# A gated recurrence and a low-rank mixer on one core: another common order of all operations, and unread matrix products joined up to 512 columns

## The chip, the core and the metric

The kernel runs on one core of a Trainium2 chip. The core has five engines, each with its own queue that it works through in order: TensorE (PE, matrix products, written to the accumulation memory PSUM; its weight loads are shown apart as PEld), VectorE (DVE, elementwise work), ScalarE (ACT, functions and copies), GpSimd (POOL) and SyncE (SP, which here issues most transfers). Transfers (DMA) move data between device memory and the on-chip memory, or within the latter. The metric is the device time of one execution in microseconds (us), the median of several runs.

## The reference

Two parts follow each other. The first is a recurrence over 768 steps with a complex decay per channel, for 4 sequences with 8 heads of 48 channels:

```python
mag = np.sqrt(a_re * a_re + a_im * a_im)
scale = np.minimum(mag, 0.999) / (mag + 1e-06)
a_re_n, a_im_n = (a_re * scale, a_im * scale)
for t in range(S):
    ar, ai = (a_re_n[:, :, t, :, None], a_im_n[:, :, t, :, None])
    new_re = ar * S_re - ai * S_im
    new_im = ar * S_im + ai * S_re
    kv = np.einsum('bhd,bhe->bhde', k[:, :, t], v[:, :, t])
    S_re, S_im = (new_re + kv, new_im)
    y[:, :, t] = np.einsum('bhd,bhde->bhe', q[:, :, t], S_re)
```

The second takes y as x, with 384 channels, mixes along the sequence through rank 32, and then applies two dense layers with a hidden width of 1536:

```python
xt = x.transpose(0, 2, 1)
h = xt @ U @ V
u = x + h.transpose(0, 2, 1)
ch = np.maximum(u @ w_ch1, 0.0) @ w_ch2
return (u + ch).astype(np.float32)
```

The weights and the low-rank factors come in double precision; the kernel makes single precision of them with integer operations on VectorE and ScalarE.

## The kernel before

The 4 x 768 steps are cut into 24 chunks of 128 steps, two to a group. For each group, `gates` (line 596) loads a_re and a_im (`load_a`, line 511), forms the logarithm of the decay in the tile GL (ScalarE and VectorE in turn, lines 624 to 645), and sums it along the chunk by matrix products with constant triangular matrices: "es ps" with `mid` and "ef ps" with `fore` (line 674, or line 670 for later groups, where the values are split in two). The exponentials of these sums weigh q and k. `of_blocks` gives sums over blocks ("tot", lines 712 and 718), which SyncE's transfers bring into the tile T (line 696). `turns_of` and `angles` do the same for the phase ("ph", lines 773 to 779, F at line 782), and `waves_of` makes cosine and sine of it.

For each chunk, `prep` (line 811) weighs q and k and transposes them on TensorE ("tr", line 834; copied out by ScalarE, line 845). `chain` (line 856) then forms products within blocks of 32 steps ("inner", lines 881 and 884), masks them into DG (line 896), copies their diagonal blocks into AT with four transfers (line 935), adds off-diagonal blocks ("corners", line 948), forms the state ("dk", line 973) and the output y (lines 1004 and 1012).

When a sequence's six chunks are done, `mixer` (line 1028) runs for its three pairs of chunks: "rank" and "mixed" for the low-rank part (lines 1047, 1066), a transposition (line 1079), the first dense layer ("up", line 1094, or, for the last five of the twelve pairs, "few" of line 1152, a scheme with fewer products and more additions), and the second ("down", lines 1241 and 1284). Weights are loaded and converted by `single` (line 529) on the side.

The order is written out. Every operation is recorded with `plan.add` under an engine and a kind; the table `ORDER` (line 28) gives for each kind and running number one place among 2,655 places that all engines share. `Plan.order` sorts by place and asserts that an operation comes after what it needs and that buffers are free; the operations are then emitted in this order, and each engine's instructions keep it. Which engine waits for which data at run time follows from the tiles that an instruction reads and writes, not from the table. The costs in the code (`c_act`, `c_dve`, `c_dma` and the numbers in `PE(...)`) are not used in `Plan.order`.

A second table, `SPARE` (line 175), puts matrix products that nobody reads in front of the operation at a given place: `ident` times `ident` into a PSUM tile "spare" of its own (line 1414), 128 columns each.

```python
out += [-1] * SPARE.get(at[n], 0) + [n]
```

Of the kernel before, what the change touches and what calls it, by code (L numbers as in the profile page):

```python
# [10 lines left out]
FP = mybir.dt.float32  # L11
# [26 lines left out]
    ("POOL", "load"): {0: [13], 1.5: [59], 2: [12], 1: [28]},  # L38
    ("DVE", "load"): {1: [40]},
# [6 lines left out]
    ("ACT", "gates"): {0: [0, 7, 6, 11, 16, 21, 23, 36, 53, 43, 44, 45, 55, 58], 1: [14, 8, 22, 29, 30, 37, 46, 54, 48, 49, 52, 57], 2: [127, 104,  # L46
# [10 lines left out]
    ("DVE", "gates"): {0: [10, 9, 17, 25, 27, 63, 24], 1: [15, 26, 33, 35, 38, 64, 41], 2: [117, 144, 151, 186], 4: [261, 313, 314, 352], 6: [427,  # L57
# [10 lines left out]
    ("ACT", "angles"): {0: [78, 87, 92, 93, 100], 1: [84, 101, 107, 111, 110], 2: [197, 202, 220, 236, 232, 238, 239, 246, 248, 249], 4: [363, 376,  # L68
# [5 lines left out]
    ("DVE", "angles"): {0: [81, 82, 90], 1: [85, 88, 103], 2: [201, 231, 245], 4: [375, 395, 419], 6: [563, 567, 571, 592, 599, 600, 636], 8: [672,  # L74
# [5 lines left out]
    ("DVE", "prep"): {0: [91, 102, 112], 1: [116, 124, 138], 2: [240, 254, 257], 3: [241, 275, 306], 4: [402, 407, 425], 5: [424, 432, 464], 6: [608,  # L80
# [159 lines left out]
def kernel(  # L240
# [24 lines left out]
    nc = tc.nc  # L265
# [44 lines left out]
    plan = Plan(places)  # L310
# [717 lines left out]
    def mixer(m):  # L1028
# [220 lines left out]
        def down_two():  # L1249
# [29 lines left out]
            def product(to, part, x, y, reads, first=True):  # L1279
# [6 lines left out]
                for half in range(2):  # L1286
                    PE(0.98, RM, lambda half=half: products(half), reads(half) + [("w2s", 0)],
                       [to + (part,), ("bank", to[1])], steps=KH)
# [181 lines left out]
```

## Time and profile before

| What | Value |
|---|---|
| median of 3 runs | 640.84 us (638.37 to 641.07) |
| the profiled execution: first to last instruction | 641.9 us |
| TensorE busy | 622.8 us in 10,516 product records |
| VectorE, ScalarE, GpSimd busy | 509.9, 396.8, 38.7 us |
| unread products (line 1414) | 294 records, 43.9 us busy, from 1.4 to 125.7 us |
| "up" of line 1094, weight loads apart | 504 records, 116.1 us busy |
| mean granted clock of TensorE | 0.992 of full speed |

A product of full-precision numbers shows as two records of the same shape. A row of the timeline gives its start, its length, engine and line, what is written from what, shapes, the number of records, and in brackets the idle time of the engine before it and what ended that. A row of waits gives who waited for whom, the time in total, how often, and the longest. A row of stretches gives, after the stretch and its length, the busy time of each engine with its records, then the granted clock as a share of full speed, the share of the transfer engines that was busy, and GB/s. The chain is the work that ended last, followed back from the end; its rows are start, length and work. TensorE's ends are modelled, so that records of one run overlap a little.

Every transfer of a_re, a_im, q, k or v is 192 KB, an issue on SyncE takes some 0.4 to 0.9 us, and the median time from issue to landing is 3.2 to 3.4 us. An AT<-DG transfer is 32 KB and lands in 2.4 us at the median.

### The profile page before, as it was taken

The page shows a single profiled execution, that of the slowest core. Times are in us where ns is not written, and L with a number is a line of the kernel's source. Part 1 is how long each engine was busy: PE and PEld are TensorE (multiplying, and loading weights), DVE is VectorE, ACT ScalarE, POOL GpSimd, SP SyncE. Part 2 cuts the span into 40 slices and gives each one's busy share as a digit, 9 for nine tenths or more (in the row PEclk, how much of TensorE's full clock was granted, in tenths as well). Part 3 has the DMA queues.
Part 4 walks back from the last instruction along what each step waited for, and adds up shares of the span by engine and source line. Part 5 has one row for each costly group of instructions (what it writes and reads, how often), then busy time and mean ns, then how long its engine had stood idle before and what let it go on. Part 6 is the DMA issues. An engine that isn't in the chain of part 4 may idle for free.

```text
span 641.9 us, 23713 instructions
## 1 busy us (share of the span) xinstructions
PE 622.8 (97%) x10516; PEld 548.0 (85%) x10516; DVE 509.9 (79%) x923; ACT 396.8 (62%) x765; POOL 38.7 (6%) x79
## 2 busy tenths in 40 slices
PE   8888997999999999999999999999999999999998
PEld 7767776686789988889988989798999998999997
DVE  6998997678999989678877868788999975473743
ACT  7898997788887787876776676687532432102020
POOL 5000000000001010010010100010000000000001
PEclk9999999799999999999999999999999999999999
DMA  7766534745233362333331332611104010000002
GB/s 202 166 148 138 125 70 102 180 119 131 51 66 69 58 126 50 67 69 68 71 77 34 75 74 43 117 37 21 32 20 81 8 42 12 7 1 1 20 1 74
DMA packets 173686, 45.76 MB, mean 71 GB/s; under 512 B 167632, under 2 KB 170384, under 8 KB 173584
## 3 DMA queue, kind: packets, MB, share of 16 engines
q1 hardware_dynamic: 171376, 39.90, 29.4%
q0 software_dynamic: 2208, 4.35, 2.0%
q8 instruction: 82, 1.34, 0.9%
q14 instruction: 20, 0.16, 0.1%
HBM read 33.59 MB, written 4.72 MB: 60 GB/s over the span
## 4 chain that ended last, share of the span: by engine, by line
PE 72%; issue 9%; ACT 7%; DMA 6%; DVE 4%; SPq 3%; POOL 0%; DVEq 0%; ACTq 0%; POOLq 0%
PE down L1284 22%; PE up L1094 11%; PE few L1152 10%; PE y L1012 3%; DMA AT<-DG 3%; PE tr L834 3%; PE dk L973 3%; PE down L1241 3%; ACT gate L374 2%; PE y L1004 2%; PE inner L884 2%; PE inner L881 2%; PE mixed L1066 1%; PE spare L1414 1%; PE tot L718 1%
## 5 line engine op out<-in xcount | busy, mean ns | idle before, releaser
L1094 PE MATMUL up<-uT,w 128*128 128x256 f32 x504 | 116.1, 383 | 0.0
L377 DVE TENSOR_TENSOR QK<-QK,T 112x512 f32<-112x512 f32 (+2 forms) x144 | 101.3, 728 | 7.1 <-PE corners L948 2.6
L1094 PEld LDWEIGHTS up<-uT,w 128*128 128x128 f32 x504 | 93.8, 190 | 12.8
L374 ACT ACTIVATE gate<-gate 128x768 f32<-128x768 f32 (+1 forms) x89 | 70.1, 798 | 8.1 <-DVE GS L768 3.1
L1284 PE MATMUL down<-w,h 128*128 128x192 f32 x396 | 73.5, 331 | 0.0
L845 ACT COPY QK<-tr 112x512 f32<-112x512 f32 x96 | 53.2, 584 | 32.2 <-PE tr L834 31.8
L1284 PEld LDWEIGHTS down<-w,h 128*128 128x128 f32 x396 | 64.1, 190 | 2.7 <-issue 1.5
L1160 ACT COPY h<-few 128x512 f32<-128x512 f32 x30 | 17.3, 586 | 60.9 <-PE few L1152 60.9
L380 DVE TENSOR_TENSOR xo<-down,xo 128x192 f32<-128x192 f32 (+1 forms) x79 | 29.9, 384 | 26.5 <-PE down L1284 26.3
L377 DVE TENSOR_TENSOR QKC<-qk,cs 128x768 f32<-128x768 f32 x48 | 45.4, 952 | 5.2 <-PE tr L834 4.5
L1414 PE MATMUL spare<-ident 128*128 128x128 f32 x294 | 43.9, 295 | 1.4 <-POOL ident masks.py:199 1.4
L1414 PEld LDWEIGHTS spare<-ident 128*128 128x128 f32 x294 | 38.1, 200 | 6.0 <-issue 2.0
L1284 PE MATMUL down<-stage 128*128 128x192 f32 x198 | 37.2, 331 | 0.0
L1152 PE MATMUL few<-gate,w 128*128 128x128 f32 x280 | 35.4, 276 | 0.0
L834 PEld LDWEIGHTS tr<-ident,QKC 64*112 64x112 f32 x768 | 25.9, 130 | 10.7 <-issue 3.3
L834 PE MATMUL tr<-ident,QKC 64*112 64x64 f32 x768 | 33.1, 223 | 1.9 <-ACT QK L845 0.8
L759 POOL DMA_DIRECT2D gate<-F x15 | 11.9, 796 | 379.1 <-DVE F L782 225.3
L1152 PEld LDWEIGHTS few<-gate,w 128*128 128x128 f32 x280 | 33.4, 192 | 0.1
L1284 PEld LDWEIGHTS down<-stage 128*128 128x128 f32 x198 | 32.1, 190 | 1.5 <-DVE stage L1276 0.6
L953 ACT COPY AT<-corners 32x128 f32<-32x128 f32 x96 | 24.2, 255 | 12.1 <-PE corners L948 10.5
L371 ACT ACT_TABLE_LOAD x24 | 30.8, 1283 | 1.1 <-PEq L1454 0.7
L1228 POOL DMA_DIRECT2D out_dram<-xo x32 | 18.5, 606 | 207.2 <-DVE xo L380 119.6
(156 smaller groups left out, 1245.9 us busy)
## 6 DMA issues: line engine op xcount, KB each, us to landing
stage<-in_moe_w_ch_dram SPq DMA_DIRECT2D x12, 768.0 KB, 4.7
gate<-in_a_im_dram SPq DMA_DIRECT2D x24, 192.0 KB, 3.3
gate<-in_a_re_dram SPq DMA_DIRECT2D x24, 192.0 KB, 3.2
VP<-in_v_dram SPq DMA_DIRECT2D x24, 192.0 KB, 3.4
qk<-in_k_dram SPq DMA_DIRECT2D x24, 192.0 KB, 3.3
qk<-in_q_dram SPq DMA_DIRECT2D x24, 192.0 KB, 3.3
AT<-DG SPq DMA_DIRECT2D x96, 32.0 KB, 2.4
T<-E SPq DMA_DIRECT2D x48, 48.0 KB, 2.5
```

The lines of the kernel that those rows point to most:

```text
L371: ACT(1.37, rank, lambda: nc.scalar.preload_act_table_set(name), writes=[TABLE])
L374: return nc.scalar.activation(out=o, in_=i, func=f, **kw)
L377: nc.vector.tensor_tensor(out=o, in0=a, in1=b, op=OP.mult)
L380: nc.vector.tensor_tensor(out=o, in0=a, in1=b, op=OP.add)
L834: nc.tensor.transpose(out=get(*ps[r])[0:DQ, h], in_=get(*qkc)[at, h].rearrange("p u d -> p (u d)")[:, 0:DQ], identity=ident[at, at], tile_ ...
L845: nc.scalar.copy(out=to, in_=a)
L953: ACT(0.36, RR, lambda r=r, u=u: nc.scalar.copy(out=get(*ATi).rearrange("p (a u) t -> p a u t", u=2)[r:r + BLK, :, u, BLK:2 * BLK], in_=ge ...
L973: nc.tensor.matmul(out=get(*dk[r])[x:end, h], lhsT=get(*ks)[at, h, x // DP, 0:end - x], rhs=get(*VPi)[at, h], start=True, stop=True, tile_ ...
L1094: nc.tensor.matmul(out=get(*ps)[:, e], lhsT=w1[:, f, (ff + e) * 128:(ff + e + 1) * 128], rhs=get(*uT)[:, f], start=(f == 0), stop=(f == KD ...
L1152: nc.tensor.matmul(out=get(*ps)[:, q], lhsT=w()[:, q * 128:(q + 1) * 128], rhs=v[0](), start=(n == 0 and q == 0), stop=True, skip_group_ch ...
L1284: nc.tensor.matmul(out=get(*to)[:, part], lhsT=x(j), rhs=y[:, j], start=(first and j == 0), stop=(j == KH - 1), skip_group_check=not first)
L1414: nc.tensor.matmul(out=spare[0], lhsT=ident, rhs=ident, start=True, stop=True)
```

## The change

All places in `ORDER` are new, for all engines and queues: the same operations with the same arguments, in another order. `SPARE` is new. Runs of unread products are joined by four into one product of up to 512 columns, whose right-hand side repeats `ident`. The second layer's products name all of w2 as read when the plan is made. There is no other edit.

The places of the first gate operations before and after (each entry is a place; the key is the chunk):

```diff
-    ("ACT", "gates"): {0: [0, 7, 6, 11, 16, 21, 23, 36, 53, 43, 44, 45, 55, 58], 1: [14, 8, 22, 29, 30, 37, 46, 54, 48, 49, 52, 57], 2: [127, 104,
+        ("ACT", "gates"): {0: [1, 4, 2, 6, 12, 13, 15, 35, 48, 42, 39, 44, 68, 76], 1: [8, 14, 24, 25, 27, 40, 36, 49, 52, 53, 54, 57], 2: [124, 81,
...
-    ("PE", "gates"): {0: [31, 32, 51], 1: [47, 50, 56], 2: [158, 161, 174, 175, 192, 191], 4: [323, 324, 335, 340, 343, 341], 6: [502, 501, 506, 507,
+        ("PE", "gates"): {0: [37, 43, 67], 1: [45, 46, 56], 2: [161, 167, 173, 174, 188, 182], 4: [318, 334, 333, 340, 354, 358], 6: [510, 501, 511,
...
-SPARE = {31: 23, 47: 2, 51: 1, 83: 11, 94: 3, 106: 7, 114: 4, 122: 5, 146: 8, 158: 1, 212: 9, 215: 3, 263: 8, 266: 4, 281: 6, 303: 2, 307: 5, 323: 1,
-        349: 2, 371: 7, 383: 1, 388: 1, 420: 6, 426: 4, 435: 1, 460: 3, 463: 1, 467: 1, 476: 6, 484: 2, 506: 1, 507: 1, 532: 1, 573: 1, 575: 2, 577:
-        2, 581: 1}
+SPARE = {37: 79, 43: 1, 45: 2, 46: 1, 56: 1, 84: 14, 93: 1, 113: 10, 116: 5, 122: 5, 127: 2, 140: 1, 144: 5, 147: 4, 173: 1, 175: 1, 205: 13, 235: 1,
+         246: 1, 255: 7, 275: 13, 287: 1, 302: 2, 305: 6, 325: 3, 340: 2, 367: 3, 376: 4, 391: 2, 416: 9, 423: 1, 433: 2, 449: 2, 455: 1, 469: 2, 488:
+         11, 492: 2, 501: 1, 510: 2, 531: 1, 571: 2, 573: 2}
...
-                    PE(0.98, RM, lambda half=half: products(half), reads(half) + [("w2s", 0)],
+                    PE(0.98, RM, lambda half=half: products(half), reads(half) + [("w2s", 0)] + ALL_W2,
...
-    def idle():
+    def idle(k):
 
         if not spare:
-            spare.append(pools["psM"].tile([128, 128], FP, tag="psM", name="spare", padded_shape=[128, 512]))
-        nc.tensor.matmul(out=spare[0], lhsT=ident, rhs=ident, start=True, stop=True)
+            spare.append(pools["psM"].tile([128, 4, 128], FP, tag="psM", name="spare"))
+        nc.tensor.matmul(out=spare[0][:, :k], lhsT=ident, rhs=ident.unsqueeze(1).to_broadcast([128, k, 128]), start=True, stop=True)
+    run = 0
     for n in plan.order():
-        (plan.ops[n][4] if n >= 0 else idle)()
+        if n < 0:
+            run += 1
+            continue
+        while run:
+            idle(min(run, 4))
+            run -= min(run, 4)
+        plan.ops[n][4]()
```

The unread products are 147 before, each an instruction of its own; after, they are worth 229 of 128 columns, in 81 instructions: 41 of 512 columns, 5 of 384, 15 of 256 and 20 of 128. The first run, ahead of the first "es ps", has 23 before and 79 after. On SyncE's queue the first transfers are, before: a_im and a_re of chunk 0, a_im and a_re of chunk 1, the constant "prefix", weights, masks, weights, v. After: a_im and a_re of chunk 0, a_re of chunk 1, "prefix", a_im of chunk 1, weights, masks, q, k, weights.

More of the change, by code (lines that the diff above doesn't have):

```diff
@@ L28 @@
 ORDER = {
[9 rows of a table removed]
-    ("POOL", "load"): {0: [13], 1.5: [59], 2: [12], 1: [28]},
-    ("DVE", "load"): {1: [40]},
[6 rows of a table removed]
-    ("ACT", "gates"): {0: [0, 7, 6, 11, 16, 21, 23, 36, 53, 43, 44, 45, 55, 58], 1: [14, 8, 22, 29, 30, 37, 46, 54, 48, 49, 52, 57], 2: [127, 104,
[10 rows of a table removed]
-    ("DVE", "gates"): {0: [10, 9, 17, 25, 27, 63, 24], 1: [15, 26, 33, 35, 38, 64, 41], 2: [117, 144, 151, 186], 4: [261, 313, 314, 352], 6: [427,
[10 rows of a table removed]
-    ("ACT", "angles"): {0: [78, 87, 92, 93, 100], 1: [84, 101, 107, 111, 110], 2: [197, 202, 220, 236, 232, 238, 239, 246, 248, 249], 4: [363, 376,
[5 rows of a table removed]
@@ L74 @@
-    ("DVE", "angles"): {0: [81, 82, 90], 1: [85, 88, 103], 2: [201, 231, 245], 4: [375, 395, 419], 6: [563, 567, 571, 592, 599, 600, 636], 8: [672,
[5 rows of a table removed]
-    ("DVE", "prep"): {0: [91, 102, 112], 1: [116, 124, 138], 2: [240, 254, 257], 3: [241, 275, 306], 4: [402, 407, 425], 5: [424, 432, 464], 6: [608,
[6 rows of a table removed]
-    ("ACT", "prep"): {0: [108, 109, 121, 120], 1: [129, 133, 148, 150], 2: [264, 265, 271, 273], 3: [300, 298, 308, 310], 4: [423, 422, 437, 436], 5:
[4 rows of a table removed]
-    ("DVE", "rest"): {0: [119, 153, 162, 166, 152, 167, 187], 1: [214, 222, 225, 242, 247, 258, 260, 267], 2: [268, 319, 321, 345, 285, 316, 320,
[8 rows of a table removed]
@@ L101 @@
-    ("DVE", "levels"): {0: [135, 140, 142, 139, 141, 143, 155], 1: [165, 185, 223, 184, 188, 190, 243], 2: [274, 292, 318, 289, 291, 305, 322], 3:
[22 rows of a table removed]
-    ("ACT", "rest"): {0: [181, 203, 177, 199, 229, 227, 226], 1: [244, 230, 237, 233, 295, 293, 296], 2: [362, 339, 357, 358, 385, 387, 374], 3: [384,
[10 rows of a table removed]
-    ("ACT", "small"): {0: [574, 585, 609, 629, 591, 631, 617, 611], 1: [730, 768, 772, 797, 751, 820, 852], 2: [971, 1072, 1119, 1109, 1051, 1116,
[4 rows of a table removed]
-    ("DVE", "small"): {0: [576, 580, 578, 717, 738], 1: [691, 727, 693, 802, 801, 884, 873, 880, 896, 919, 958, 939, 894, 942, 947, 963, 946, 962,
[25 rows of a table removed]
@@ L166 @@
-    ("POOL", "small"): {0: [917, 739], 1: [1100, 1099, 1101], 2: [1265, 1229, 1264], 3: [1654, 1502, 1503], 4: [1701, 1655, 1700], 5: [1897, 1920,
-        1921], 6: [2246, 2110, 2111], 7: [2372, 2298, 2304], 8: [2621, 2610, 2623], 9: [2612, 2620, 2622], 10: [2613, 2611, 2619]},
-    ("POOL", "angles"): {6: [595], 8: [678, 713], 10: [846, 918], 12: [1095], 14: [1257, 1278], 16: [1449, 1485], 18: [1653], 20: [1854, 1894], 22:
-        [2020, 2066]},
-    ("ACT", "levels"): {6: [774], 7: [814], 8: [933], 9: [1009], 10: [1145], 11: [1144], 12: [1335], 13: [1334], 14: [1551], 15: [1536], 16: [1750],
-        17: [1743], 18: [1930], 19: [1931], 20: [2143], 21: [2150], 22: [2320], 23: [2319]},
@@ L172 @@
-    ("DVE", "mixing"): {7: [1991, 2012, 2051, 2068, 2070, 1992, 2014, 2086, 2087, 2102, 2103, 2106, 2050]},
-}
-SPARE = {31: 23, 47: 2, 51: 1, 83: 11, 94: 3, 106: 7, 114: 4, 122: 5, 146: 8, 158: 1, 212: 9, 215: 3, 263: 8, 266: 4, 281: 6, 303: 2, 307: 5, 323: 1,
-        349: 2, 371: 7, 383: 1, 388: 1, 420: 6, 426: 4, 435: 1, 460: 3, 463: 1, 467: 1, 476: 6, 484: 2, 506: 1, 507: 1, 532: 1, 573: 1, 575: 2, 577:
-        2, 581: 1}
[9 rows of a table added]
+        ("POOL", "load"): {0: [10], 1: [51], 1.5: [217], 2: [28]},
@@ new lines @@
+        ("DVE", "load"): {1: [61]},
[6 rows of a table added]
+        ("ACT", "gates"): {0: [1, 4, 2, 6, 12, 13, 15, 35, 48, 42, 39, 44, 68, 76], 1: [8, 14, 24, 25, 27, 40, 36, 49, 52, 53, 54, 57], 2: [124, 81,
[10 rows of a table added]
+        ("DVE", "gates"): {0: [5, 16, 17, 21, 22, 55, 18], 1: [19, 20, 26, 32, 41, 71, 58], 2: [123, 143, 151, 198], 4: [264, 288, 312, 337], 6: [418,
[10 rows of a table added]
+        ("ACT", "angles"): {0: [77, 85, 95, 94, 102], 1: [79, 100, 108, 110, 109], 2: [199, 211, 231, 251, 247, 252, 250, 258, 259, 262], 4: [366,
[5 rows of a table added]
+        ("DVE", "angles"): {0: [78, 83, 90], 1: [80, 87, 101], 2: [203, 244, 253], 4: [381, 401, 410], 6: [559, 568, 569, 585, 595, 596, 635], 8:
[5 rows of a table added]
@@ new lines @@
+        ("DVE", "prep"): {0: [75, 103, 106], 1: [107, 119, 141], 2: [248, 254, 260], 3: [266, 280, 304], 4: [406, 409, 413], 5: [445, 454, 463], 6:
[6 rows of a table added]
+        ("ACT", "prep"): {0: [114, 115, 120, 121], 1: [135, 131, 154, 155], 2: [273, 274, 281, 279], 3: [301, 298, 316, 320], 4: [421, 420, 426, 427],
[4 rows of a table added]
+        ("DVE", "rest"): {0: [128, 156, 164, 202, 166, 172, 195], 1: [208, 213, 236, 249, 256, 261, 265, 268], 2: [283, 322, 331, 365, 291, 310, 317,
[8 rows of a table added]
+        ("DVE", "levels"): {0: [126, 138, 146, 130, 139, 142, 159], 1: [158, 184, 204, 171, 197, 207, 227], 2: [282, 294, 311, 290, 300, 309, 323], 3:
[22 rows of a table added]
@@ new lines @@
+        ("ACT", "rest"): {0: [201, 185, 186, 200, 239, 214, 215], 1: [257, 242, 271, 243, 293, 297, 296], 2: [348, 347, 346, 343, 372, 373, 375], 3:
[10 rows of a table added]
+        ("ACT", "small"): {0: [570, 581, 597, 633, 606, 622, 641, 612], 1: [721, 782, 755, 796, 761, 840, 844], 2: [974, 1065, 1126, 1102, 1053, 1115,
[4 rows of a table added]
+        ("DVE", "small"): {0: [572, 578, 577, 731, 736], 1: [689, 734, 691, 826, 822, 823, 851, 869, 894, 897, 896, 935, 895, 899, 952, 968, 963, 971,
[25 rows of a table added]
+        ("POOL", "small"): {0: [901, 902], 1: [999, 900, 1152], 2: [1280, 1279, 1347], 3: [1506, 1421, 1504], 4: [1748, 1730, 1731], 5: [2002, 1914,
@@ new lines @@
+        2003], 6: [2175, 2162, 2174], 7: [2358, 2312, 2349], 8: [2458, 2573, 2626], 9: [2553, 2569, 2574], 10: [2641, 2615, 2627]},
+        ("POOL", "angles"): {6: [594], 8: [688, 724], 10: [847, 898], 12: [1101], 14: [1244, 1278], 16: [1450, 1505], 18: [1648], 20: [1862, 1905],
+        22: [2020, 2058]},
+        ("ACT", "levels"): {6: [762], 7: [817], 8: [937], 9: [1017], 10: [1137], 11: [1145], 12: [1341], 13: [1337], 14: [1539], 15: [1564], 16:
+        [1753], 17: [1755], 18: [1930], 19: [1937], 20: [2159], 21: [2149], 22: [2318], 23: [2309]},
@@ L180 @@
+        ("DVE", "mixing"): {7: [2001, 2015, 2010, 2060, 2078, 2004, 2005, 2071, 2079, 2109, 2098, 2111, 2056]},
+}
+SPARE = {37: 79, 43: 1, 45: 2, 46: 1, 56: 1, 84: 14, 93: 1, 113: 10, 116: 5, 122: 5, 127: 2, 140: 1, 144: 5, 147: 4, 173: 1, 175: 1, 205: 13, 235: 1,
+         246: 1, 255: 7, 275: 13, 287: 1, 302: 2, 305: 6, 325: 3, 340: 2, 367: 3, 376: 4, 391: 2, 416: 9, 423: 1, 433: 2, 449: 2, 455: 1, 469: 2, 488:
+         11, 492: 2, 501: 1, 510: 2, 531: 1, 571: 2, 573: 2}
 class Plan:
```

246 rows, old and new, of the table ORDER are left out of this document.

## The prediction, on record before the changed kernel ran

> **What bounds the kernel now.** I read the page's first two parts, then four stretches of the span engine by engine, then the start of TensorE's timeline, then the list of waits with TensorE as the waiting engine, and last the chain for prices.
>
> ```profile
> span 641.9 us, 23713 instructions
> PE 622.8 (97%) x10516; PEld 548.0 (85%) x10516; DVE 509.9 (79%) x923; ACT 396.8 (62%) x765; POOL 38.7 (6%) x79
> ...
> PEclk9999999799999999999999999999999999999999
> ```
>
> TensorE (PE) is busy for 622.8 of 641.9 us, and it takes its instructions in order. So the span is a plain sum of four things: products that the output needs, products that nobody reads (line 1414), idle time, and time lost while the granted clock is low (the 7 in the eighth slice). Only the last three depend on the order. The stretches show where they lie. The columns are the length, then busy time of PE, weight loads, VectorE (DVE), ScalarE (ACT) and POOL, then the clock.
>
> ```profile
> 0.00:9.54 9.54, 7.18 (x46) 7.02 (x47) 5.38 (x19) 6.49 (x13) 5.84 (x21) 1.00 0.84 220
> 9.54:126.10 116.56, 104.36 (x2324) 82.17 (x2324) 104.89 (x178) 99.56 (x188) 3.22 (x12) 0.96 0.57 131
> 126.10:625.00 498.90, 497.44 (x8062) 445.27 (x8063) 392.96 (x712) 290.78 (x567) 26.41 (x41) 1.00 0.26 54
> 625.00:641.90 16.90, 13.82 (x86) 13.53 (x84) 6.65 (x16) 0.00 (x0) 3.20 (x6) 1.00 0.21 70
> ```
>
> From 126.1 us on PE is idle for 1.5 us in 498.9, so no order can win much there; the last stretch ends with 3.1 us of a last addition and store, which stay. Everything in play lies before 126.1: 2.36 us idle up to 9.54, 12.2 us idle from there on (116.56 - 104.36), and the unread products.
>
> ```profile
> 1.42 7.18 PE L1414 MATMUL spare<-ident 128*128 128x128 f32 x46 [1.42 <-POOL ident masks.py:199]
> 9.54 0.88 PE L674 MATMUL es ps<-GL,mid 128*128 128x384 f32 x2 [0.94 <-DVE GL L380]
> 14.98 2.72 PE L1414 MATMUL spare<-ident 128*128 128x128 f32 x22
> 80.09 0.49 PE L1414 MATMUL spare<-ident 128*128 128x128 f32 x2
> ```
>
> Each product is two records. The first 23 unread products fill the wait for the first decay rates (GL); the first product that counts, "es ps" of line 674, starts at 9.54, after 0.94 us of waiting for VectorE. The last unread product ends at 126.1.
>
> ```profile
> PE y L1004 <- DMA AT<-DG: 3.8, 4, 1.6
> PE y L1004 <- DMA gate<-in_a_re_dram: 1.1, 1, 1.1
> PE ph L776 <- issue: 1.1, 1, 1.1
> PE inner L884 <- issue: 1.1, 2, 0.6
> PE inner L881 <- issue: 0.7, 1, 0.7
> ```
>
> Of the 12.2 us, then, 4.9 end with a transfer, 2.9 with "issue" (nothing that the profile shows), and the other 4.4 with results of VectorE and ScalarE.
>
> **The change, part by part.** *The first run of unread products.* It grows from 23 to 79, and in the built program PE begins with nineteen products of 512 columns and one of 384 before the same "es ps". Prices of one pass: 22 records take 2.72 us and 2 take 0.49, so 128 columns cost (2.72 - 0.49) / 20 = 0.1115 us. Wider ones come from two rows of the chain:
>
> ```profile
> 146.31 2.58 PE down L1241 x8
> 170.44 5.18 PE up L1094 x24
> ```
>
> 384 columns cost 2.58 / 8 = 0.3225, 256 cost 5.18 / 24 = 0.216. The step is 0.107 per 128 columns, so 512 should cost 0.429; bounds are this and four times 0.1115 = 0.446. The run then takes 19 x 2 x 0.429 + 2 x 0.3225 = 16.9 us. The 46 records of before took 7.18 where 46 x 0.1115 is 5.1: the start is slower by some 1.9 us, which stays. So the run lasts from 1.42 to 1.42 + 16.9 + 1.9 = 20.2, and "es ps" moves from 9.54 to 20.2: **+10.7 us**. Does its input move as well? In the new order SyncE issues the second a_im load behind the constant "prefix" (one issue, 0.76 us) and VectorE does two steps of the second chunk before it ends the first chunk's GL, so GL is ready near 10 us. The move of that load is hidden by the run; without it, it would cost about 0.8. What is queued behind: on ScalarE the second exponential of "es ps" stands ahead of the second chunk's Ln, and VectorE's sum for that chunk's GL waits for this Ln. So both stop soon after 12 us until "es ps" is there; only three steps of the weight conversion fit in before.
>
> *The other unread products.* 124 become 150, in 61 instructions (22, 4, 15 and 20 of 512, 384, 256 and 128 columns). Before: 124 x 0.223 = 27.7. After: 22 x 0.858 + 4 x 0.645 + 15 x 0.432 + 20 x 0.223 = 32.4. **+4.7 us**. Joining saves only some 0.04 us per four.
>
> *The needed products.* The same number. Left without the unread ones, the order on PE changes from one kind of product to another 417 times instead of 401. In the chain a run of "up" that ends in a change shows 2.79 us against 2.59, so 16 more changes cost 0 to 3.2 us. I take **0.5**, since most of that 0.2 is the drain, under which the next product already runs.
>
> *Idle time of PE after "es ps", I, now 12.2.* It cannot be below zero; with nothing gained it stays 12.2. The 4.9 behind transfers: the loads have 10.7 us of head start, and the AT<-DG copies of line 935 stand in another order on SyncE's queue, past V<-UV and T<-E copies; between 0 and 4.9, I take 1.6. The 2.9 of "issue": no part of the change names it, 0 to 2.9, I take 2.0. The 4.4 behind results: the waits have about as many unread products ahead of them as before (11 becomes 14, 7 becomes 10, 4 becomes 5), I take 2.7. Together **6.3**. VectorE agrees with a number of this size: by mean durations of its kinds the new order leaves it 101.8 us of work between "es ps" and the last unread product, before 104.5 in 116.6. With I = 6.3 that stretch is 116.6 - 12.2 - 3.9 + 4.7 + 6.3 = 111.5 us, so VectorE idles 9.7 us against 12.1.
>
> *The clock, T.* From 110.2 to 121.5 the granted clock was 0.55. Pieces of the chain there against the same pieces elsewhere: y of line 1012 1.76 and 1.88 for 1.07, dk 1.87 for 1.07, rank 1.44 and 1.32 for 0.78, y of line 1004 1.04 for 0.61: 3.9 us lost. Just before, PE was busy for 0.32 us of 1.7 (108.5 to 110.2), after another wait of 1.13 us. If the transfers behind these two waits come in time, T is 0, otherwise 3.9. I take 0.
>
> [...]
>
> *The added dependency (ALL_W2), the planner's new waits, the wider "spare" tile.* They issue nothing: the first is read by the planner alone, and the tile filled a bank before too. Nothing, with no cover needed. The moved output stores on POOL and the order after 126.1 meet a PE with 1.5 us of idle in 499: -1.5 to about +2, I take 0.
>
> Sum, on the profiled span: 641.9 + 10.7 + 4.7 + 0.5 - 12.2 - 3.9 + I + T = 641.7 + I + T. With 6.3 and 0: 648.0. That execution lies 1.1 us over the median of the runs (640.84), so the **forecast is 646.9 us**.
>
> **The rivals.** *The clock falls again and the idle time stays.* For it: the waits for AT<-DG come from an SP queue that stays as crowded, and the stop of VectorE and ScalarE near 12 us leaves them the same work to do later. Against: loads land long before they are used. Price: I 10 and T 3.9, 655.6 in span, 654.5 us.
>
> *Not slower: the unread products cover the waits.* One mechanism: during the 10.7 us the loads land, and the 32.4 us of later unread products lie just where PE would wait, so that what was 12.2 idle and 3.9 clock is bought with 15.4 of products. For it: 0.94 us of wait before "es ps" and the DMA waits must go. Against: 79 products cover a wait of about 8 us, so 10 of the 15.4 lie where no wait was. It decides from I + T below 3.9 on. Price: I 2.0, T 0, 642.6 us.
>
> *Faster: needed products get shorter.* It would take 10 us out of the 499 in which PE shows 1.5 us of idle; the count of changes speaks against it. About 636 us.
>
> *It does not do what it says:* joined products that run no faster than four single ones add 41 x 2 x 0.017 = 1.4 us; inside the forecast.
>
> **How the numbers follow.** Chances: forecast 0.59 (I + T from 4 to 10), clock and idle 0.18, not slower 0.18, faster 0.05. A measurement here can tell about 0.5%, 3.2 us, from no change: slower is above 644.0, 0.59 + 0.18 = 0.77; within, 0.18; faster, below 637.6, 0.05. The range runs from I + T = 1 (641.6) to I 10 with T 3.9 (654.5). It takes in the bounds of the joined price.
>
> **What would show it.** The first "es ps" near 20.2 us, with no wait for GL in front of it and VectorE idle before it. Pairs of 512 columns at 0.86 us. A last unread product between 130 and 137 us and about 516 us after it. PE idle of 4 to 9 us between the two, and a clock digit of 9 in every slice. I am wrong if "es ps" starts before 15 us, if the needed products from there to the end are shorter by more than 2 us, or if nearly no idle time is left.

## The result, and the profile after

The changed kernel takes 644.93 us (median of 17 runs, 642.85 to 649.39); the kernel before, on the same chips, takes 641.07 (17 runs, 638.12 to 648.04). The ratio is 1.0073, with a 95% interval of 1.0055 to 1.0091: slower by 0.7%, 4.7 us, and outside the 0.5% that is called no change here. The forecast was 646.9 us, with a range of 641.6 to 654.5. A ratio leaves out the runs that took more than 1.5% longer than the fastest of the same kernel, which matters for E6 below.

The page of the changed kernel, its first line and its busy times:

```profile
span 643.5 us, 23479 instructions
PE 633.6 (98%) x10384; PEld 535.4 (83%) x10384; DVE 510.2 (79%) x923; ACT 398.5 (62%) x765; POOL 39.1 (6%) x79
```

TensorE is busy for 10.8 us more than before (633.6 against 622.8), and the span has grown by only 1.6. So most of the added work took the place of waiting. The four stretches, cut at the same events as before (the first "es ps", the last unread product), show where. Columns: stretch, its length, busy time with records of PE, weight loads, VectorE, ScalarE and POOL, the granted clock, the busy share of the transfer engines, GB/s.

```profile
0.00:21.40 21.40, 19.97 (x40) 8.79 (x41) 7.29 (x23) 7.39 (x14) 9.02 (x32) 1.00 0.64 155
21.40:126.65 105.25, 101.77 (x2193) 67.87 (x2191) 101.36 (x171) 97.90 (x185) 0.00 (x0) 1.00 0.57 130
126.65:625.00 498.35, 496.45 (x8058) 443.66 (x8058) 393.28 (x712) 293.20 (x567) 28.98 (x45) 1.00 0.27 56
625.00:643.50 18.50, 15.38 (x97) 15.08 (x96) 8.23 (x19) 0.00 (x0) 1.07 (x2) 1.00 0.11 37
```

The first stretch is 11.9 us longer than before (21.40 against 9.54). The second is 11.3 us shorter (105.25 against 116.56), although more unread products stand in it (by their passes 4.7 us more): its idle time fell from 12.2 to 3.5 us (105.25 - 101.77), and the granted clock is 1.00 where it was 0.96. From the last unread product to the end it is 516.9 us against 515.8. The sum, 11.9 - 11.3 + 1.1, is the 1.6 us by which the spans differ. VectorE and ScalarE do nearly the same work in the second stretch as before (101.4 and 97.9 us), in less time.

The start of TensorE's timeline, after. A row is start, length, engine, line, work and shapes, number of records, and in brackets the idle time before it and what ended that.

```profile
1.43 20.14 PE L1414 MATMUL spare<-ident 128*128 128x512 f32 x40 [1.43 <-POOL ident masks.py:199]
21.40 0.81 PE L674 MATMUL es ps<-GL,mid 128*128 128x384 f32 x2
...
23.89 0.88 PE L674 MATMUL es ps<-GL,mid 128*128 128x384 f32 x2 [0.38 <-DVE GL L380]
```

"es ps" has no bracket: it waits for nothing but the run of unread products in front of it. VectorE's own timeline shows the other side.

```profile
9.18 0.56 DVE L380 TENSOR_TENSOR GL<-GL,gate 128x384 f32<-128x384 f32 x1
...
11.36 0.56 DVE L560 TENSOR_SCALAR w<-w 128x768 uint32<-128x768 uint32 x1
23.18 0.56 DVE L380 TENSOR_TENSOR GL<-GL,gate 128x384 f32<-128x384 f32 x1 [11.27 <-ACT gate L374]
```

GL of the first chunk is complete at 9.74, 11.7 us before TensorE reads it, and VectorE then stands still for 11.27 us, until ScalarE has the first "es ps". The waits of TensorE, after (total, how often, longest):

```profile
PE y L1004 <- DMA AT<-DG: 0.8, 1, 0.8
PE tr L834 <- ACT QK L845: 0.7, 3, 0.3
...
PE spare L1414 <- issue: 0.4, 1, 0.4
PE ph L776 <- issue: 0.4, 1, 0.4
```

The 4.9 us behind transfers have become 0.8, the 2.9 us of "issue" 1.2 in all.

One profile is one execution, and that of the kernel before is not a usual one. Its mean granted clock is 0.992; of the 50 runs of that kernel beside the experiments, 23 have 0.999 or 1.000 and 8 have 0.992 or less. The 17 runs of the changed kernel have 0.997 to 1.000. So the low clock that the change removes in the two profiles is absent from many runs of the kernel before anyway.

### The profile page after: what moved, and what is told of

Read it like the earlier page. It is cut to its first block, busy times and chain, and to the rows that moved or that the text cites. A ratio compares the mean times of both kernels' runs of the same rounds, so it can differ in the third digit from the quotient of the medians.

```text
span 643.5 us, 23479 instructions
## 1 busy us (share of the span) xinstructions
PE 633.6 (98%) x10384; PEld 535.4 (83%) x10384; DVE 510.2 (79%) x923; ACT 398.5 (62%) x765; POOL 39.1 (6%) x79
## 4 chain that ended last, share of the span: by engine, by line
PE 87%; DVE 8%; issue 2%; ACT 1%; DMA 1%; SPq 0%; POOL 0%; DVEq 0%; POOLq 0%
PE down L1284 24%; PE up L1094 18%; PE few L1152 11%; PE spare L1414 5%; PE tr L834 3%; PE y L1012 3%; PE dk L973 3%; PE inner L884 3%; PE down L1241 2%; PE inner L881 2%; PE y L1004 2%; PE tot L718 2%; DVE QKC L377 2%; PE mixed L1066 1%; DVE QK L377 1%
## 5 line engine op out<-in xcount | busy, mean ns | idle before, releaser
L377 DVE TENSOR_TENSOR QK<-QK,T 112x512 f32<-112x512 f32 (+1 forms) x144 | 102.3, 730 | 7.1 <-PE inner L881 3.3
L1414 PE MATMUL spare<-ident 128*128 128x512 f32 (+3 forms) x162 | 62.2, 506 | 1.8 <-POOL ident masks.py:199 1.4
L1414 PEld LDWEIGHTS spare<-ident 128*128 128x128 f32 x162 | 29.4, 196 | 27.9 <-issue 21.9
L834 PE MATMUL tr<-ident,QKC 64*112 64x64 f32 x768 | 32.4, 222 | 0.9 <-ACT QK L845 0.7
L374 ACT ACTIVATE es<-es ps 128x384 f32<-128x384 f32 x48 | 21.9, 491 | 17.8 <-PE es ps L674 11.3
```

The source lines that it names most:

```text
L374: return nc.scalar.activation(out=o, in_=i, func=f, **kw)
L377: nc.vector.tensor_tensor(out=o, in0=a, in1=b, op=OP.mult)
L834: nc.tensor.transpose(out=get(*ps[r])[0:DQ, h], in_=get(*qkc)[at, h].rearrange("p u d -> p (u d)")[:, 0:DQ], identity=ident[at, at], tile_ ...
L1414: nc.tensor.matmul(out=spare[0][:, :k], lhsT=ident, rhs=ident.unsqueeze(1).to_broadcast([128, k, 128]), start=True, stop=True)
```

## The experiments

Nine kernels. They differ in the unread products alone, or in whether the old or the new order is taken. A ratio is against the kernel before, run beside it. The runs of E1 to E4, of E5 to E7, and of E8 and E9 were made together, each group on one chip.

**E1: the changed kernel with a first run of 24.** The run is then six products of 512 columns.

```diff
-SPARE = {37: 79, 43: 1, 45: 2,
+SPARE = {37: 24, 43: 1, 45: 2,
```

> The changed kernel with 24 instead of 79 unread products in its first run. Theory (the 79 hold back the first es ps and everything behind it, and the rest of the new order is by itself better than the old one): 55 products fewer at 0.2145 us take 11.8 us off 644.9, and 0 to 4 us of idle time come back, so 633 to 637 us, with es ps near 10 us. Rival (the long run only gives the loads their head start, and that is why the stretch after es ps is short, 105 us instead of 117): the stretch grows back to 114 to 117 us and the time is 641 us or more.

Measured: 642.89 us, ratio 0.9995 (0.9967 to 1.0024). The theory missed, and the time is that of the rival, though not its stretch: from "es ps" to the last unread product it is 111.7 us, short of the 114 to 117 that the rival asked for. "es ps" is back at 9.88 us, 11.5 earlier than in the changed kernel, but the time came down by only 5.0 us (0.78% of 641). Some 6.5 us had been taken back elsewhere. The waits of TensorE in this kernel name where to look:

```profile
PE spare L1414 <- issue: 2.2, 1, 2.2
PE corners L948 <- issue: 2.0, 1, 2.0
```

These two waits are not in the changed kernel at all, and the profile names no other engine or transfer that ends them. All "issue" waits make 5.2 us here, 1.2 in the changed kernel.

**E2: the kernel before with a first run of 79.**

```diff
-SPARE = {31: 23, 47: 2, 51: 1,
+SPARE = {31: 79, 47: 2, 51: 1,
```

> The kernel before with 79 instead of 23 unread products in its first run, nothing else. Theory: 56 products of 0.223 us are 12.5 us, of which at most 2 come back, 651 to 653.5 us. Rival (head start): the stretch after es ps shrinks by 8 to 12 us, and the time is 642 to 646 us.

Measured: 651.96 us, ratio 1.0129 (1.0086 to 1.0172). 56 more unread products at the start make the old order slower by 8.3 us (give or take 2.8). The time is the theory's and the rival fell: in its profile "es ps" stands at 21.73, 12.2 later, and the waits for AT<-DG are 4.6 us, about what they were. By the ratio some 4 us of the 12.2 came back, more than the theory's 2, and the head start does not pay for the rest. The profile is of the slowest run, 658.03 us, with 17.1 us at half clock.

**E3: the kernel before with joined products only.** The old `ORDER` and the old `SPARE`, with the change's `idle(k)` and loop; 6 products in front.

```diff
-        (plan.ops[n][4] if n >= 0 else idle)()
+        if n < 0:
+            run += 1
+            continue
+        while run:
+            idle(min(run, 4))
+            run -= min(run, 4)
+        plan.ops[n][4]()
```

> The kernel before with its unread products joined up to 512 columns, old order and old counts. Theory: 92 instructions fewer, each 0.0115 us of fixed cost, 1.1 us at most, half of it given back as idle time: 640 to 641 us, no change that can be told. Rival (wide products hurt: the clock rises later, and a needed product behind a wide one starts later): 642.5 to 645 us.

Measured: 638.89 us, ratio 0.9947 (0.9922 to 0.9973): 3.4 us faster, more than the prediction's arithmetic of columns gives. Its profile has idle 10.2 us between "es ps" and the first "up" where the kernel before has 12.2, and no stretch at a low clock, where the kernel before has 10.2 us at half clock. The clock is not what made the difference, though: among runs with a granted clock of 0.999 or 1.000 the medians are 637.7 us (7 of 12 runs of E3) and 640.8 (10 of 23 of the kernel before), 3.0 us apart.

**E4: the changed kernel with single products.**

```diff
-            idle(min(run, 4))
-            run -= min(run, 4)
+            idle(min(run, 1))
+            run -= min(run, 1)
```

> The changed kernel with its 229 unread products single, 128 columns each, in the same places. Theory (joining is worth its fixed cost alone): 148 more instructions at 0.0115 us, 1.7 us more at most, less what the earlier rise of the clock gives back at the start (1.2 us): 644.5 to 646.6 us. Rival (the wide products are what costs in the changed kernel): 640 to 643 us.

Measured: 652.42 us, ratio 1.0150 (1.0110 to 1.0191). Both theories missed: unjoined, the changed kernel is slower by another 0.8%. "issue" is 4.2 us in it (changed kernel: 1.2), with one wait of 2.40 us:

```profile
PE spare L1414 <- issue: 3.6, 2, 2.4
```

The columns are the same, and the fixed costs are 1.7 us at most. So the number of products on TensorE, or the place that each of them gets by it, must matter apart from the columns.

**E5: a first run of 24 columns' worth in as many products as the changed kernel has there, twenty.** Sixteen of 128 columns and four of 256. Every later product then has the same running number in TensorE's program as in the changed kernel.

```diff
-SPARE = {37: 79, 43: 1, 45: 2,
+SPARE = {37: 24, 43: 1, 45: 2,
...
-    run = 0
+    run, first = 0, [2] * 4 + [1] * 16
...
-            idle(min(run, 4))
-            run -= min(run, 4)
+            k = first.pop() if first else min(run, 4)
+            idle(k)
+            run -= k
```

> The changed kernel with 24 columns' worth of unread products (of 128 columns each) in its first run, but in 20 instructions, as many as in the changed kernel: sixteen of 128 columns and four of 256. TensorE's idle time with no releaser but issue stood in the earlier runs where its instruction count reaches the same place in a block of 256 (two records per product, 156 to 184 after a multiple of 256). Theory (the stalls are instruction blocks that arrive late, and the count of instructions ahead decides whether such a border falls into a dense burst): the stalls of the run with 24 in 6 instructions (2.2, 1.2 and 2.0 us) are gone, at most 1.5 us of issue idle time stay, the clock stays up, 636 to 639 us. Rival (the long first run helps by the head start of the loads): the stalls come as in that run, 641 to 644 us.

Measured: 634.14 us, ratio 0.9890 (0.9855 to 0.9924), a little better than the theory; the rival fell, so E1 had the rival's time for another reason. Its start:

```profile
1.42 7.22 PE L1414 MATMUL spare<-ident 128*128 128x128 f32 x40 [1.42 <-POOL ident masks.py:199]
10.14 0.88 PE L674 MATMUL es ps<-GL,mid 128*128 128x384 f32 x2 [1.50 <-DVE GL L380]
```

and its stretches to the same event as before (columns as above):

```profile
0.00:10.14 10.14, 7.22 (x40) 6.70 (x41) 5.23 (x19) 6.29 (x12) 6.92 (x27) 1.00 0.88 209
10.14:116.50 106.36, 101.74 (x2192) 67.98 (x2192) 103.30 (x176) 99.04 (x188) 2.66 (x6) 1.00 0.60 140
```

The second stretch is the changed kernel's but for 1.1 us: the same records, the same busy time of TensorE (101.74 and 101.77), clock 1.00, 4.6 us idle against 3.5. The first is 11.3 us shorter. From 0.9890 to 1.0073 is 1.8%, 11.7 us (give or take 2.5, from the two intervals): that is what the longer first run costs, and the waits that it saves later are worth about 1 us. (The spans of the two profiled executions are 8.9 us apart; E5's is of its slowest run.)

**E6: the first run of 79 in 70 products instead of 20.** Else as E5.

```diff
-    run = 0
+    run, first = 0, [4] * 3 + [1] * 67
```

A product shows as two records with two weight loads. 50 more products are 200 more records and loads, and 6 products (E1) and 70 (E6) are 24 and 280, equal in the remainder by 256.

> The changed kernel with the same 79 columns' worth in its first run, but in 70 instructions instead of 20, 67 of 128 columns and three of 512, so that all later borders of 256 instructions fall where they fell with 24 in 6 instructions. Fixed costs of the 50 more are 0.6 us; the first es ps stays near 21 us. Theory (late instruction blocks): issue idle time of 3 to 6 us and stretches of half clock appear, 647 to 651 us. Rival (head start of the loads): as the changed kernel, 644 to 646 us.

Measured: 655.66 us over six runs that spread from 648.11 to 662.43; 651.1 us over the four that the ratio takes, ratio 1.0171 (1.0111 to 1.0231). With the same columns in front as the changed kernel and the same order, it is 1.0% slower, give or take 0.6. The direction is the theory's, and 651.1 is at the upper end of its range. Part of it is the clock: the two runs with 0.995 and 1.000 took 648.11 and 648.43 us, the four with 0.992 to 0.977 took 653.72 to 662.43. The profile is of a run of 657.6. Where TensorE waits in it, from its timeline:

```profile
116.76 0.38 PE L948 MATMUL corners<-QK 112*32 112x32 f32 x22
119.14 0.31 PE L948 MATMUL corners<-QK 112*32 112x32 f32 x10 [2.00 <-issue]
```

and in E1, whose first run has 64 products fewer:

```profile
62.93 1.14 PE L973 MATMUL dk<-VP,QKC 64*64 64x48 f32 x64
66.25 1.67 PE L1414 MATMUL spare<-ident 128*128 128x512 f32 x4 [2.17 <-issue]
...
103.15 0.38 PE L948 MATMUL corners<-QK 112*32 112x32 f32 x22
105.54 0.31 PE L948 MATMUL corners<-QK 112*32 112x32 f32 x10 [2.01 <-issue]
```

Both stop for 2.0 us in the middle of one group of 32 records, after the same 22nd record of it. The profile names no input that was late for either. Counted from the beginning, products and weight loads together, the stop comes after 3,740 in E1 and 3,996 in E6: the remainder by 256 is 156 in both. The other waits for "issue" over half a microsecond in E1 and E6 lie at remainders of 156 to 168. A queue that the profile calls "instruction" moves packets of 16,384 bytes; one starts at 103.21 us in E1, and TensorE goes on at 105.54. Which engine a packet is for the profile does not say. After the wait of 2.17 us E1 has 3.4 us at half clock. E6 has 6.8 us of it beside a wait of 1.86 us for an AT<-DG transfer, and 17.1 us after its wait of 2.00, to be seen in the line of the granted clock in 40 slices of its page,

```profile
PEclk9999799689999999999999999999999999999999
```

which in E5 is

```profile
PEclk9999999999999999999999999999999999999999
```

E1, E5, E6 and the changed kernel make a table of two by two, all in the new order and with the same 150 unread products later:

| first run | remainder of E1 and E6 | remainder of the changed kernel and E5 |
|---|---|---|
| 24 | 0.9995 | 0.9890 |
| 79 | 1.0171 | 1.0073 |

The columns in front cost 1.8% in either column of the table. The place of the later products costs 1.0 to 1.1% in either row (give or take 0.5 and 0.6), some 6.5 us, stops and the low clock behind them together, and has nothing to do with columns. So E1 missed because it undid the cost of the columns and moved the places as well. The mere number of products in front does not explain the table: 20 are better than 6, and 70 are worse than 20.

**E7: the changed kernel with 24 in front and no other unread product.**

```diff
-SPARE = {37: 79, 43: 1, 45: 2,
...
+SPARE = {37: 24}
```

> The changed kernel with 24 unread products in its first run (in 6 instructions) and none of the 150 later ones. They take 32 us of TensorE's time in a stretch in which it is otherwise starved. Theory (they stand where TensorE would wait, and buy the full clock): the 32 us turn into idle time, the clock is at half for most of the stretch up to the first up, which costs needed products there up to 15 us more: 642 to 655 us. Rival (they hold up needed products more than they help): 628 to 638 us.

Measured: 648.09 us, ratio 1.0107 (1.0070 to 1.0145). 150 later products, 32.4 us of passes, taken away make the kernel 1.1% slower than E1 (1.0107 against 0.9995), some 7 us. One stretch of this kernel and its line of the clock:

```profile
10.00:115.00 105.00, 74.93 (x1813) 55.56 (x1814) 93.84 (x160) 89.32 (x166) 2.63 (x6) 0.76 0.58 132
```

```profile
PEclk9777796699999999999999999999999999999999
```

TensorE idles 30 us of 105 and the granted clock is 0.76. All five runs have a mean clock of 0.947 to 0.952, where those of E1 have 0.976 to 0.997: the later unread products keep the clock up. The price of 7 us holds for all that they do, for leaving them out also moves the places of the needed products.

**E8: E3 with its first run in twenty products.** The old order.

```diff
-    run = 0
+    run, first = 0, [2] * 3 + [1] * 17
```

> The kernel before with joined unread products (old order, old counts), but its first run of 23 in 20 instructions, seventeen of 128 columns and three of 256, instead of 6. If the place of the instruction blocks' borders matters in any order, TensorE's idle time behind issue (2.7 us with 6) changes by 1 us or more either way, and the time moves with it by 1 to 4 us from about 639. If the borders hurt only at the places that the new order gave, the time stays at 638 to 640 us.

Measured: 638.56 us, ratio 0.9951 (0.9923 to 0.9979), the same as E3. In the old order, moving the places (6 products in front in E3, 20 here) changed nothing in the time that can be told apart, although the waits for "issue" in its profile add up to 3.9 us against 2.7: one sign of the expectation came, the other did not.

**E9: the changed kernel with 24 in thirteen products.** A place between E1 and E5.

```diff
-SPARE = {37: 79, 43: 1, 45: 2,
+SPARE = {37: 24, 43: 1, 45: 2,
...
-    run = 0
+    run, first = 0, [1] * 2 + [2] * 11
```

> The changed kernel with 24 columns' worth in its first run in 13 instructions, half way between 6 (643 us) and 20 (634 us). Borders fall 14 records later in the needed products than with 20 and 14 earlier than with 6. Theory (late instruction blocks; it depends on what stands just ahead of each border): a time between 632 and 644 us that goes with the issue idle time, 634 to 636 us if that is below 2 us and 640 or more if it is above 4. Rival (the loads' head start, or the number of instructions by itself): 637 to 640 us whatever the issue idle time is.

Measured: 637.40 us, ratio 0.9938 (0.9920 to 0.9957), between the two. Its waits of TensorE again hold two that nothing in the profile ends:

```profile
PE dk L973 <- issue: 2.4, 1, 2.4
PE inner L881 <- issue: 1.6, 1, 1.6
```

They come after 1,960 and 3,484 products and loads, remainders 168 and 156, and 6.8 us at half clock come with the second. Together the "issue" waits are 4.8 us, for which the theory asked for 640 us or more. The profiled run took 640.53, but the median is in the rival's range, so the theory's rule missed here and E9 does not decide. With the same columns and the same order, 6, 13 and 20 products in front give 0.9995, 0.9938 and 0.9890.

The parts are links of one chain from the kernel before to the changed one, so that they must add up. Joining alone (E3) is -0.5%. From the old order to the new, each with its own later unread products, both joined and with 23 and 24 in twenty products in front (E8 to E5), is -0.6%, give or take 0.4. The longer first run is +1.8%. Together +0.7%, the measured change. E5, the change with its first run kept short, is faster than both kernels: 634.14 us against 639.87 of the kernel before beside it.

## Why the prediction was right, point by point

| Step | Forecast | Measured |
|---|---|---|
| first "es ps" | 20.2 us (+10.7) | 21.40 (+11.9) |
| one pass of 512 columns | 0.429 us | 0.429 to 0.430 |
| other unread products | 32.4 us (+4.7) | passes 32.4; from start to next start 39.0 (+3.7) |
| needed products, from "es ps" to the end | -3.9 (clock) + 0.5 | 574.6 us (-5.8) |
| idle after "es ps", to the last unread product | 6.3 us | 3.5 |
| of it behind transfers; "issue" | 1.6; 2.0 | 0.8; 1.2 |
| time lost to the clock | 0 | 0 |
| last unread product | 130 to 137 us | 126.65 |
| from there to the end | about 516 us | 516.9 |
| span | 648.0 us | 643.5 |

**The first run.** Right, and it decides: the first useful product waits for unread ones alone, and E5 against the changed kernel prices this at 11.7 us, near the 10.7 of the forecast. The mis-sized part is the slow start, "1.9 us, which stays". In the changed kernel the first six passes of 512 columns take 0.853 us or more each, and full speed comes at 7.45 us; before, passes of 128 take 0.213 us or more until 5.2. In E5 full speed comes at 4.96 us and in E9 at about 7.0, so the length of the slow start varies by 2.5 us, and a constant for it was wrong.

**The other unread products.** The passes cost what was forecast. But the product behind a run starts later than its last pass ends: counted from the start of each record to the start of the next, idle time left out, the 124 of before hold TensorE for 35.3 us and the 150 of after for 39.0, so the term was 3.7 and not 4.7. "Joining saves only some 0.04 us per four" was wrong as a price of joining: E3 measures -3.4 us. In columns it saves next to nothing; 2.1 us less idle time is what its profile shows, and where the rest comes from is open.

**The needed products.** The term "I take 0.5" had the wrong sign. Counted in the same way from the first "es ps" to the end, the same 10,222 needed records take 580.4 us before, 577.0 in E3, which has the old order and the full clock, and 574.6 after. So 3.4 us went with the clock, near the 3.9 of the sum, and 2.4 with the new order. The prediction had named more than 2 us of this as a sign of being wrong, and the sign came by a little: the mechanism of its rival "faster" was at work, at a quarter of the 10 us asked for. The ground given for the 0.5, that the next product runs under the end of the last, rests on ends that the profile models: in the kernel before, an "es ps" record that starts at 104.83 us and lasts 0.34 has the next product start at 105.00.

**Idle time and clock.** The direction was right and the size of I too large by 2.8 us: transfers cost 0.8 and not 1.6, "issue" 1.2 and not 2.0, results 1.5 and not 2.7 (3.5 less 0.8 and 1.2). T was taken as 0 and is 0, though nothing in the working made that more than a choice. I + T is 3.5, just outside the 4 to 10 to which the forecast tied its chance; the last unread product ends before 130 us and the idle time is under the 4 to 9 us, so that two of the signs named beforehand did not come.

**The step that failed without harm** is 'The 2.9 of "issue": no part of the change names it'. Both parts do. They set how many products stand in front of each other one, and this decides what stops for "issue" (E1, E6, E9: 1.6 to 2.4 us at one place). The changed kernel lies at a good place, E1 and E6 at a bad one; 6.5 us between them was not in the forecast or its bounds (2.9). That the change fell on a good place was luck.

**From span to run.** "That execution lies 1.1 us over the median" compared a span with a time. A run's time is 1.7 to 1.9 us more than its span in the changed kernel (645.24 and 643.5) and 1.7 to 3.0 in the runs of the kernel before beside the experiments, so the profiled execution of before was a run of 643.6 us at least, 2.8 over the median of 640.84; it holds 10.2 us at half clock. The mistake helped, and that was luck: the span was forecast 4.5 us too long, the time only 2.0. Of the 4.5 us, 2.8 are I, 2.4 the needed products with the clock (5.8 less instead of 3.4) and 1.0 the unread ones; the start, 1.2, and 0.5 us more of idle time behind the last unread product go the other way.

**The rivals.** "Not slower" named a mechanism that works: later unread products cover waits and hold the clock (E7), and with I at 3.5 and T at 0 its condition, I + T below 3.9, was just met. That the 26 more of them (150 for 124) bought the 8.7 us of idle time and the clock is not shown, for the order changed with them, and E3 has no stretch at half clock with the old number. Its 642.6 asked for an I of 2.0, and the 11.9 us in front come on top; under nearly all of these there was no wait (E5 waits 1.50 us for GL). "Clock and idle stay" is near to what the same columns do at another place (E6: 651.1 us, or 655.66 over all runs, against its 654.5), for a reason that it did not name. "Faster" had a mechanism that did come, worth 2.4 us; the kernel as a whole would have needed a short first run to be faster (E5).

## What to carry to other kernels

A filler in front of the first useful work is worth little more than the wait that it covers: of 11.3 us too many in the new order about 1 came back later, of 12.2 in the old one about 4. Read when the input is ready (9.74 us here) and end it there. Judge an edit that adds or removes instructions by two runs or more that place the later ones differently, or by keeping the count: 14 unread products more in front, with the same columns in the same order, were worth 1.0% (E1 to E5). Where two terms can't be parted in one run, two sizes by two places part them.

## What the hardware showed that was not expected

**TensorE stops at places that repeat every 256 products and loads.** In E1, E6 and E9 the waits for "issue" of 1.6 to 2.4 us all stand at remainders 156 to 168, and so does the one of 2.40 in E4. Not every such wait does: one of 1.17 us in E4 stands at 182 and one of 3.60 in E7 at 104. Two waits of the kernel before lie at remainders of 156 and 164:

```profile
108.50 0.32 PE L1004 MATMUL y<-VP,AT 64*64 64x48 f32 x4 [1.13 <-DMA gate<-in_a_re_dram]
110.22 0.67 PE L1004 MATMUL y<-VP,AT 64*64 64x48 f32 x28 [1.40 <-DMA AT<-DG]
```

The first is put down to a transfer whose data y does not read. They are the waits that the prediction put down to late transfers and behind which its clock fell (10.2 us at half clock), so these may have been such stops too; no run parts the two. The queue that the profile calls "instruction" has a like count: its packets of 16,384 bytes are 82 in the kernel before, 81 in the changed one and 80 in E7, beside 21,032, 20,768 and 20,468 products and loads of TensorE, some 256 to a packet in each. That a packet is a block of TensorE's instructions, and that a stop is a block that comes late, is the author's estimate from these counts; no run shows it. The cost differs from kernel to kernel: the longest "issue" wait is 0.41 us in the changed kernel and 2.0 to 2.4 us in E1, E4, E6 and E9. Why TensorE stops at one such place and not at another was not settled; that wide products let a block last longer fits E3 and E4, but was only argued, and E8 shows that the place need not matter.

**The clock can fall after a single wait of about 2 us, and need not.** In E1 a wait of 2.17 us is followed by 3.4 us at half clock, and in E6 one of 2.00 by 17.1 us. No fall follows the wait of 2.01 us in E1, of 2.40 in E4 or of 2.43 in E9. Away from the span's end, the stretches at half clock in the kernel before, E1, E2, E4, E6 and E9 are 3.4, 6.8, 10.2, 13.7 or 17.1 us long, one to five times 3.4.
